# Reordering the loads, casts and weight parts of an attention and max-out kernel's first 60 microseconds

## Chip, cores and metric

The kernel runs on one core of one Trainium2 chip. The metric is the device time of one execution in microseconds (us).

## What is computed

The reference is a softcap attention followed by a feed-forward layer with a maximum of two products. Cut to what matters:

```python
batch, n_heads, seq, head_dim = (8, 12, 448, 64)          # q, k, v: float32, cap = 30
scores = (1 / sqrt(head_dim)) * q @ k.T                   # per batch and head, 448 x 448
scores = cap * tanh(scores / cap)
attn = softmax(scores)
x = (attn @ v).transpose(0, 2, 1, 3).reshape(3584, 768)   # heads side by side
out = maximum(x @ w1, x @ w2) @ w_out                     # w1, w2: 768 x 1024, w_out: 1024 x 768
```

## The kernel before

**Units and groups.** Two heads of one batch element make a unit ("pair"); there are 48 of them. Three units make a **group**, the portion in which q, k and v are loaded: groups 0 to 15, called the first, second, third and so on. The attention loop takes two units per step `t`, so a step may need two groups: step 3 is the first that reads group 2 (units 6 and 7), and step 4 the first that reads group 3 (unit 9).

**Road of q and k.** `load(g, what)` (L113) issues the DMAs from SP's queue into a float32 staging tile, `kr`, `qr` or `vr` in the profile. `raw_of` (L105) takes that tile from a pool: two buffers each for k and q, used in turn, and a single one for v. For groups 0 and 1 a load is one DMA, from group 2 on it is two (q) or three (k, v): the first 384 rows of each head, then the other 64. `cast` (L140) converts the tile to bf16, most often on GpSimd; k and q go into `kqf`, one of two tiles by the group's parity, v into `vp` and `vl`, also two of each. Then k and q have to be transposed to have the head dimension on the partitions. For groups 0 and 1 TensorE does it (`transposes`, L255, L267 and L268), from group 2 on a DMA does, `cross(g)` (L271), issued from SP, from `kqf` into `qkT`.

**Road through attention.** `scores(t, p)` (L282, matmuls of L295 and L300) computes a quarter of a step's scores in PSUM and lets ScalarE take the tanh (L301, L303). `ex` (L305, L308) takes the exponential. `add` (L316) forms partial sums of exponentials on VectorE, `total` (L337) sums over the keys on TensorE and inverts on VectorE, `values` (L358) multiplies with v, and `normalize` (L386) writes x, transposed, as `xT`.

**Road of the weights.** The maximum is computed as `x @ w2 + relu(x @ (w1 - w2))`, so `wd = w1 - w2` and `wm = w2 @ w_out` are needed. w1 and w2 come in six parts each. `load_w2(c)` (L209) and `load_wo(f)` (L200) are issued from GpSimd's queue and convert to bf16 on the way; w2's parts land in a tile that the profile calls `gT`. `load_w1(c)` (L214) is issued from SP's queue in float32, into tiles called `osb` and `xT`. `subtract(c)` (L218, L219) forms one part of wd on GpSimd. `turn_w2(c)` (L223) transposes w2 on TensorE, and `premultiply` (L231, L237) and `premultiply_first` (L518, L524) multiply it with w_out.

**The feed-forward part.** `moe(b)` (L392, matmuls of L400, L412 and L415) works on one batch element after the other.

**What sets the order.** Each engine executes its instructions in the order in which the program issues them, and this order is written out by hand: first a prologue for steps 0 to 2 (L474 to L592), then the loop over `t`. Matmuls of the weights and of the feed-forward part are kept as generators in a list and drawn into the attention's gaps by `F(n)` (L444), n at a time, counted and not timed. Three queues matter around the change: SP's instructions (loads of q, k, v, w1, the transposes, later the stores), GpSimd's instructions (issues of w2 and w_out, casts, subtractions), and the DMA engines, which serve both. An instruction that waits, for a buffer or for data, holds everything behind it on its engine.

**Order on the two engines in question.** On SP: k and q of groups 0 and 1, v of group 0, v of group 1 (its one buffer is free when group 0's v is cast, by GpSimd and VectorE), k and q of group 2, w1 parts 0 and 1, `cross(2)`, w1 parts 2 to 5, k, q of group 3, v of group 2, and in step 2 `cross(3)`. On GpSimd, after the first w2 parts and w_out: cast of group 1's k and q, w2 parts 2 to 5, half of group 0's v, group 1's v, group 2's k and q, subtractions 0 and 1, subtractions 2 and 3, group 3's k and q, subtractions 4 and 5, group 2's v.

Of the kernel before, what the change touches and what calls it, by code (L numbers as in the profile page):

```python
# [10 lines left out]
def kernel(  # L11
# [11 lines left out]
    nc = tc.nc  # L23
    f32 = mybir.dt.float32
# [4 lines left out]
    B, H, S, D = q.shape  # L29
# [3 lines left out]
    P = 128  # L33
    KC, FC = DM // P, DF // P
    NP = H // 2
    N = B * NP
    L = 3
    NQ = N // 2
    Q0 = 4 * P
    NJ = 3  # L40
# [55 lines left out]
    raw = {}  # L96
# [4 lines left out]
    def rows(t, b, h0, h1):  # L101

        return t[b, h0:h1, :, :].rearrange("h (r j) d -> (h r) (j d)", j=R7)

    def raw_of(g, what):  # L105
        if (g, what) not in raw:
            raw[g, what] = stage.tile([P, 2 * L * NJ * D + (2 * L if what == "q" else L) * D], f32, name=what + "r", bufs=1 if what == "v" else 2)
        t = raw[g, what]
        m = t[:, : 2 * L * NJ * D].rearrange("p (h c) -> p h c", c=NJ * D)
        l = t[:, 2 * L * NJ * D :].rearrange("p (h d) -> p h d", d=D)  # L110
        return t, m, l

    def load(g, what, n0=0, n1=L):  # L113
        b, p = divmod(g * L, NP)
        h0, h1 = 2 * (p + n0), 2 * (p + n1)
        src = {"k": k, "q": q, "v": v}[what]
        t, m, l = raw_of(g, what)
        if g < NT:
            nc.sync.dma_start(
                out=t[:, n0 * S : n1 * S].rearrange("p (n c) -> p n c", c=S),  # L120
                in_=rows(src, b, h0, h1).rearrange("(n p) c -> p n c", p=P),
            )
            return
        nc.sync.dma_start(
            out=m[:, 2 * n0 : 2 * n1, :],
            in_=src[b, h0:h1, 0 : NJ * P, :].rearrange("h (p j) d -> p h (j d)", j=NJ),
        )
        if what == "q":
            nc.sync.dma_start(
                out=l[half(b), 2 * n0 : 2 * n1, :],  # L130
                in_=src[b, h0:h1, NJ * P : S, :].rearrange("h p d -> p h d"),
            )
        else:
            for par in range(2):
                nc.sync.dma_start(
                    out=l[64 * par : 64 * par + 64, n0:n1, :],
                    in_=src[b, h0 + par : h1 : 2, NJ * P : S, :].rearrange("h p d -> p h d"),
                )

    def cast(eng, g, what, n0=0, n1=L, halves=(0, 1)):  # L140

        b = g * L // NP
        x, m, l = raw_of(g, what)
        if what == "v" and g < NT:

            x = x[:, : L * S].rearrange("p (n c) -> p n c", c=S)
            for h in halves:
                r = slice(64 * h, 64 * h + 64)
                for a in range(2):
                    eng.tensor_copy(  # L150
                        vp[g % 2][64 * a : 64 * a + 64, h::2, :, :].rearrange("p n j d -> p n (j d)"),
                        x[r, :, NJ * D * a : NJ * D * (a + 1)],
                    )
                eng.tensor_copy(vl[g % 2][r, :, r], x[r, :, 2 * NJ * D :])
            return
        if what == "v":
            eng.tensor_copy(  # L157
                vp[g % 2][:, 2 * n0 : 2 * n1, :, :].rearrange("p h j d -> p h (j d)"), m[:, 2 * n0 : 2 * n1, :]
            )
            for par in range(2):  # L160
                r = slice(64 * par, 64 * par + 64)
                eng.tensor_copy(vl[g % 2][r, n0:n1, r], l[r, n0:n1, :])
            return
        if g < NT:

            x = x[:, n0 * S : n1 * S].rearrange("p (n c) -> p n c", c=S)
            if what == "q":
                eng.tensor_copy(flat(g)[:, n0:n1, Q0 : Q0 + S], x)
                return
            eng.tensor_copy(flat(g)[:, n0:n1, : NJ * P], x[:, :, : NJ * P])  # L170
            for par in range(2):
                r = slice(64 * par, 64 * par + 64)
                eng.tensor_copy(kf[g % 2][r, n0:n1, 3, r], x[r, :, NJ * P :])
            return
        o = b % 2 if what == "q" else 0
        t = (kf if what == "k" else qf)[g % 2]
        eng.tensor_copy(  # L177
            t[:, n0:n1, o : o + NJ, :].rearrange("p n j (h d) -> p n h j d", h=2),
            m[:, 2 * n0 : 2 * n1, :].rearrange("p (n h) (j d) -> p n h j d", h=2, d=D),
        )  # L180
        if what == "q":
            eng.tensor_copy(
                t[half(b), n0:n1, 3 * (1 - o), :],
                l[half(b), 2 * n0 : 2 * n1, :].rearrange("p (n h) d -> p n (h d)", h=2),
            )
        else:
            for par in range(2):
                r = slice(64 * par, 64 * par + 64)
                eng.tensor_copy(t[r, n0:n1, 3, r], l[r, n0:n1, :])
# [19 lines left out]
    def load_w2(c):  # L209
        nc.gpsimd.dma_start(out=w2b[:, c, :], in_=x_rows(moe_w2, c))  # L210
# [7 lines left out]
    def subtract(c, eng=nc.vector):  # L218
        eng.tensor_sub(wd_sb[:, c, :], w1_in[c], w2b[:, c, :])  # L219
# [51 lines left out]
    def cross(g):  # L271

        nc.sync.dma_start_transpose(
            out=qkT_of(g).rearrange("p n j c -> p (n j) c"), in_=kqf[g % 2].rearrange("p n j c -> p (n j c)")
        )
# [228 lines left out]
    ex(0, 3)  # L504
    cast(nc.gpsimd, 1, "k")
    cast(nc.gpsimd, 1, "q")
    for c in range(2, KC):
        load_w2(c)
    cast(nc.gpsimd, 0, "v", halves=(1,))
    load(1, "v")  # L510
    load(2, "k")
    load(2, "q")
    load_w1(0)
    load_w1(1)

# [2 lines left out]
    def premultiply_first(f0, f1):  # L518
        if f0 == 0:
            first[0] = pv_psum.tile([P, 512], f32, name="pv")  # L520
            first[1] = pv_psum.tile([P, 512], f32, name="ss")
        for f in range(f0, f1):
            for half in range(2):
                nc.tensor.matmul(  # L524
                    first[half][:, : DM // 2],
                    w2T[0][:, f * P : (f + 1) * P],
                    wo_sb[:, f, half * (DM // 2) : (half + 1) * (DM // 2)],
                    start=(f == 0), stop=(f == FC - 1),
                )
        if f1 == FC:  # L530
            for half in range(2):
                nc.vector.tensor_copy(
                    wm_sb[:, 0, half * (DM // 2) : (half + 1) * (DM // 2)], first[half][:, : DM // 2]
                )
# [7 lines left out]
    scores(1, 0)  # L542
    transposes(3)
    cast(nc.vector, 0, "v", halves=(0,))
    cast(nc.gpsimd, 1, "v")
    cast(nc.gpsimd, 2, "k")
    cast(nc.gpsimd, 2, "q")
    premultiply_first(0, 2)
    scores(1, 1)
    ex(1, 0)  # L550
# [6 lines left out]
    scores(1, 3)  # L557
    ex(1, 2)
    cross(2)
    for c in range(2, KC):  # L560
        load_w1(c)
    load(3, "k")
    load(3, "q")
    load(2, "v")
    premultiply_first(6, 8)
    for c in range(1, KC):
        if c + 1 < KC:
# [9 lines left out]
    for t in range(1, NQ):  # L577
        i = 2 * t
        more = t + 1 < NQ
        if t > 1 and more:  # L580
            scores(t + 1, 0)
        if t > 1:
            ex(t, 3)
            F(6)
        if t in crosses:
            cross(crosses[t])
        if t == 2:
            subtract(2, nc.gpsimd)
            subtract(3, nc.gpsimd)
            cast(nc.gpsimd, 3, "k")  # L590
            cast(nc.gpsimd, 3, "q")
            cross(3)  # L592
            subtract(4, nc.gpsimd)
            subtract(5, nc.gpsimd)
        if t == 3:
            cast(nc.gpsimd, 3, "v")
        if t > 2:
            extra(i)
        F(8 if t > 1 else 0)
        add(t, 1, 0)  # L600
        F(2 if t > 1 else 0)
        if more:
            scores(t + 1, 1)
            ex(t + 1, 0)
        F(4)
        add(t, 1, 1)
        F(4)
        if t == 2:
            cast(nc.gpsimd, 2, "v")
            load(3, "v")  # L610
        add(t, 0, 2)
        F(4)
        add(t, 1, 2)
        F(4)
        if more:
            scores(t + 1, 2)
            ex(t + 1, 1)
            F(5)
            add(t + 1, 0, 0)
        if t == 1:  # L620
            subtract(0, nc.gpsimd)
            subtract(1, nc.gpsimd)
        if t == 2:
            extra(4)
            extra(5)
        if t > 2:
            extra(i + 1)
        F(5)
        total(t)
        if more:  # L630
            scores(t + 1, 3)
            ex(t + 1, 2)
            add(t + 1, 0, 1)
        else:
            F(12)
        normalize(t, values(t))
        if t % 3 == 2:
            fill_q.append(moe(t // 3))
        F(3)
# [34 lines left out]
```

## Time and profile before

| What | Value |
|---|---|
| Time, median of 13 runs (range) | 364.16 us (362.19 to 366.56) |
| Profiled execution, its time | 366.56 us |
| Its span, first to last instruction | 364.8 us |
| Mean granted TensorE clock | 0.991 |
| Busy: TensorE, ScalarE, VectorE, GpSimd | 336.2, 281.7, 239.2, 112.5 us |
| DMA bytes moved, mean rate | 61.79 MB, 169 GB/s |
| Last exponential of ScalarE ends | 307.7 us |

A profile row names the engine (PE is TensorE, ACT ScalarE, DVE VectorE, POOL GpSimd, SP the engine that issues most DMAs, with a q for its issues), the line of the kernel, the operation, and the tiles as out<-in with their shapes. In a timeline the row starts with its start and duration in us, and its bracket holds the idle time of the engine before it and what ended that. The granted clock is a share of TensorE's full clock. The DMA share is the busy share of the 16 DMA engines, which can come out somewhat above 1.

### The profile page before, as it was taken

The page shows a single profiled execution, that of the slowest core. Times are in us where ns is not written, and L with a number is a line of the kernel's source. Part 1 is how long each engine was busy: PE and PEld are TensorE (multiplying, and loading weights), DVE is VectorE, ACT ScalarE, POOL GpSimd, SP SyncE. Part 2 cuts the span into 40 slices and gives each one's busy share as a digit, 9 for nine tenths or more (in the row PEclk, how much of TensorE's full clock was granted, in tenths as well). Part 3 has the DMA queues.
Part 4 walks back from the last instruction along what each step waited for, and adds up shares of the span by engine and source line. Part 5 has one row for each costly group of instructions (what it writes and reads, how often), then busy time and mean ns, then how long its engine had stood idle before and what let it go on. Part 6 is the DMA issues. An engine that isn't in the chain of part 4 may idle for free.

```text
span 364.8 us, 6775 instructions
## 1 busy us (share of the span) xinstructions
PE 336.2 (92%) x2710; PEld 163.6 (45%) x2710; DVE 239.2 (66%) x410; ACT 281.7 (77%) x265; POOL 112.5 (31%) x154
## 2 busy tenths in 40 slices
PE   4889695989979999999999999999999999899996
PEld 2434252434534444344534454445444545455563
DVE  4254465886778686788678767886787667833421
ACT  4998696779989999899998999999999999000000
POOL 6624759471181109110911091109210100000000
PEclk9998999899999999999999999999999999999999
DMA  7999696896778486949593963995392111012022
GB/s 259 247 214 340 128 359 154 237 287 159 215 209 192 100 257 207 231 94 265 163 244 78 260 183 96 260 275 160 92 245 78 43 45 75 13 45 87 0 88 86
DMA packets 103200, 61.79 MB, mean 169 GB/s; under 512 B 62336, under 2 KB 98176, under 8 KB 103168
## 3 DMA queue, kind: packets, MB, share of 16 engines
q1 hardware_dynamic: 101216, 58.21, 57.3%
q0 software_dynamic: 1952, 3.15, 4.7%
q8 instruction: 21, 0.34, 0.4%
q14 instruction: 11, 0.09, 0.1%
HBM read 42.47 MB, written 11.01 MB: 147 GB/s over the span
## 4 chain that ended last, share of the span: by engine, by line
PE 42%; ACT 33%; DVE 12%; DMA 3%; SPq 3%; issue 2%; POOL 2%; ACTq 0%; POOLq 0%; DVEq 0%
PE mm L400 16%; ACT expo L308 15%; ACT tanh L301 15%; PE mm L415 8%; PE mm L412 6%; PE s L300 4%; ACT tanh L303 3%; DVE esum L327 3%; DVE esum L329 3%; PE ss L366 2%; DVE esum L331 2%; DVE gT L404 2%; PE pv L366 2%; DMA qkT<-kqf 1%; DVE osb L419 1%
## 5 line engine op out<-in xcount | busy, mean ns | idle before, releaser
L308 ACT ACTIVATE expo<-tanh 128x1792 bf16<-128x1792 bf16 (+1 forms) x96 | 144.8, 1509 | 0.1
L301 ACT ACTIVATE tanh<-s 128x896 bf16<-128x896 f32 x144 | 124.3, 914 | 20.4 <-PE s L300 18.5
L415 PE MATMUL mm<-wo_sb,gT 128*128 128x384 bf16 x448 | 86.3, 327 | 0.0
L400 PE MATMUL mm<-xT,wd_sb 128*128 128x448 bf16 x384 | 79.9, 353 | 4.6 <-DVE gT L404 2.3
L412 PE MATMUL mm<-wm_sb,xT 128*128 128x384 bf16 x336 | 66.8, 326 | 0.7 <-DVE osb L419 0.7
L157 POOL CAST vp<-vr 128x1152 bf16<-128x1152 f32 x14 | 16.6, 1184 | 142.3 <-PE ss L366 115.7
L415 PEld LDWEIGHTS <-gT 128*128 128x128 bf16 x448 | 42.1, 98 | 35.1 <-issue 8.8
L419 DVE COPY osb<-mm 128x384 f32<-128x384 f32 x56 | 31.0, 554 | 38.2 <-PE mm L415 38.0
L400 PEld LDWEIGHTS <-wd_sb 128*128 128x128 bf16 x384 | 35.9, 98 | 44.0 <-issue 13.4
L300 PE MATMUL s<-qkT 64*128 64x448 bf16 x288 | 43.1, 369 | 12.8 <-DMA qkT<-kqf 7.6
L329 DVE TENSOR_TENSOR esum<-expo 128x896 bf16<-128x896 bf16 x42 | 32.7, 779 | 29.9 <-ACT expo L308 29.2
L404 DVE TENSOR_SCALAR gT<-mm 128x448 bf16<-128x448 f32 x64 | 39.5, 620 | 13.5 <-PE mm L400 13.1
L412 PEld LDWEIGHTS <-xT 128*128 128x128 bf16 x336 | 31.5, 98 | 26.0 <-issue 5.8
L327 DVE TENSOR_TENSOR esum<-esum,expo 64x896 bf16<-64x896 bf16 x42 | 31.1, 740 | 1.1
L331 DVE TENSOR_TENSOR esum<-esum,expo 128x896 bf16<-128x896 bf16 x42 | 29.6, 704 | 0.2
L303 ACT ACTIVATE tanh<-s 128x896 bf16<-128x896 f32 x24 | 22.0, 916 | 6.4 <-PE s L295 5.9
L300 PEld LDWEIGHTS <-qkT 64*128 64x128 bf16 x288 | 9.7, 95 | 36.1 <-issue 25.4
L366 PEld LDWEIGHTS <-vp 128*32 128x32 bf16 x576 | 13.5, 97 | 19.9 <-issue 12.5
L352 DVE STREAM_TRANSPOSE st<-ss 128x448 f32<-128x448 f32 x24 | 15.5, 646 | 9.4 <-PE ss L350 5.4
L366 PE MATMUL ss<-expo,vp 128*32 128x448 bf16 x288 | 18.0, 355 | 2.2 <-DVE st L352 2.1
L366 PE MATMUL pv<-expo,vp 128*32 128x448 bf16 x288 | 18.6, 365 | 0.0
L177 POOL CAST kqf<-qr 128x1152 bf16<-128x1152 f32 x14 | 17.4, 1240 | 1.7 <-DMA qr<-in_q_dram 0.9
(69 smaller groups left out, 263.7 us busy)
## 6 DMA issues: line engine op xcount, KB each, us to landing
kr<-in_k_dram SPq DMA_DIRECT2D x14, 576.0 KB, 4.8
qr<-in_q_dram SPq DMA_DIRECT2D x14, 576.0 KB, 5.9
vr<-in_v_dram SPq DMA_DIRECT2D x14, 576.0 KB, 5.2
out_dram<-osb SPq DMA_DIRECT2D x20, 384.0 KB, 2.7
out_dram<-osb SPq DMA_DIRECT2D x16, 192.0 KB, 2.8
osb<-in_moe_w_dram SPq DMA_DIRECT2D x4, 512.0 KB, 5.5
gT<-in_moe_w_dram POOLq DMA_DIRECT2D x6, 256.0 KB, 9.9
wo_sb<-in_moe_w_out_dram POOLq DMA_DIRECT2D x4, 384.0 KB, 15.2
```

What stands on the lines that cost most here:

```text
L300: nc.tensor.matmul(s[:, h, :S], k0[r, j * P : (j + 1) * P], qTn[r, :])
L301: nc.scalar.activation(tanh[t, p][:, 2 * m : 2 * m + 2, :], s[:, :, :S], AF.Tanh, scale=scale / cap)
L308: nc.scalar.activation(expo[t, p], tanh[t, p][:, 0:n, :], AF.Exp, scale=float(cap))
L327: nc.vector.tensor_add(d, d, expo[t, 2][r, :, :])
L329: nc.vector.tensor_add(d, e_of(t, ab, 1 if ab else 0), e_of(t, ab, 2 if ab else 1))
L331: nc.vector.tensor_add(d, d, e_of(t, ab, 0 if ab else 2))
L366: nc.tensor.matmul(ps[r, :S], vp[g % 2][:, 2 * n + h, j, u::2], e_of(t, ab, j)[:, h, :], start=(j == 0), stop=False,)
L400: nc.tensor.matmul(ps[:, :S], wd_sb[:, c, f * P : (f + 1) * P], x[:, c, cs], start=(c == 0), stop=(c == KC - 1))
L404: nc.vector.tensor_relu(g[:, f, cs], ps[:, :S])
L412: nc.tensor.matmul(ps[:, : DM // 2], x[:, c, ts], wm_sb[:, c, hs], start=(c == 0), stop=False)
L415: nc.tensor.matmul(ps[:, : DM // 2], g[:, f, ts], wo_sb[:, f, hs], start=False, stop=(f == FC - 1))
L419: nc.vector.tensor_copy(osb[:, hs], ps[:, : DM // 2])
```

## The change

The third group's k and q get the second buffer of their pool instead of the first: an additional tile is taken from the pool and left unused, so that group 2 shares buffers with group 1, and group 3 with group 0. Group 2's q and k are loaded ahead of group 1's v and cast ahead of it. w2's parts 4 and 5 are issued behind these casts. Group 3's k and q are loaded ahead of w1's parts 2 to 5, and cast behind subtractions 0 and 1, which move from step 1 into the prologue; the other four subtractions come behind those casts, in step 2. No instruction is added or removed.

```diff
+    def raw_tile(what):
+        return stage.tile(
+            [P, 2 * L * NJ * D + (2 * L if what == "q" else L) * D], f32, name=what + "r", bufs=1 if what == "v" else 2
+        )
...
-            raw[g, what] = stage.tile([P, 2 * L * NJ * D + (2 * L if what == "q" else L) * D], f32, name=what + "r", bufs=1 if what == "v" else 2)
+            raw[g, what] = raw_tile(what)
...
     def load(g, what, n0=0, n1=L):
         b, p = divmod(g * L, NP)
+        if g == 2 and what != "v":
+            raw.setdefault((2, what, "skipped"), raw_tile(what))
...
     cast(nc.gpsimd, 1, "k")
     cast(nc.gpsimd, 1, "q")
-    for c in range(2, KC):
-        load_w2(c)
+    load_w2(2)
+    load_w2(3)
     cast(nc.gpsimd, 0, "v", halves=(1,))
+    load(2, "q")
+    load(2, "k")
     load(1, "v")
-    load(2, "k")
-    load(2, "q")
     load_w1(0)
     load_w1(1)
...
     cast(nc.vector, 0, "v", halves=(0,))
+    cast(nc.gpsimd, 2, "q")
+    cast(nc.gpsimd, 2, "k")
+    load_w2(4)
+    load_w2(5)
     cast(nc.gpsimd, 1, "v")
-    cast(nc.gpsimd, 2, "k")
-    cast(nc.gpsimd, 2, "q")
...
     cross(2)
+    load(3, "k")
+    load(3, "q")
     for c in range(2, KC):
         load_w1(c)
-    load(3, "k")
-    load(3, "q")
     load(2, "v")
+    subtract(0, nc.gpsimd)
+    subtract(1, nc.gpsimd)
+    cast(nc.gpsimd, 3, "k")
+    cast(nc.gpsimd, 3, "q")
...
         if t == 2:
-            subtract(2, nc.gpsimd)
-            subtract(3, nc.gpsimd)
-            cast(nc.gpsimd, 3, "k")
-            cast(nc.gpsimd, 3, "q")
             cross(3)
-            subtract(4, nc.gpsimd)
-            subtract(5, nc.gpsimd)
+            for c in range(2, KC):
+                subtract(c, nc.gpsimd)
...
-        if t == 1:
-            subtract(0, nc.gpsimd)
-            subtract(1, nc.gpsimd)
```

## The prediction

> **What bounds the kernel now.** I read the page's busy shares first. TensorE is busy for nine tenths of the span, and its instruction order is fixed in the program, so the question is where its few idle microseconds lie.
>
> ```profile
> PE 336.2 (92%) x2710; PEld 163.6 (45%) x2710; DVE 239.2 (66%) x410; ACT 281.7 (77%) x265; POOL 112.5 (31%) x154
> ```
>
> The TensorE timeline (start, duration, instructions, idle time before them and what ended it) shows two long holes, both in the first 70 us and both ended by a transpose that the DMA engines make, qkT<-kqf: 3.48 us before 44.06 (the third group's scores) and 4.08 us before 62.86 (the fourth group's).
>
> ```profile
> 40.09 0.49 PE L237 MATMUL mm<-wo_sb,w2T 128*128 128x384 bf16 x2
> 44.06 0.55 PE L300 MATMUL s<-qkT 64*128 64x448 bf16 x4 [3.48 <-DMA qkT<-kqf]
> ...
> 62.86 0.55 PE L300 MATMUL s<-qkT 64*128 64x448 bf16 x2 [4.08 <-DMA qkT<-kqf]
> 63.34 4.11 PE L237 MATMUL mm<-wo_sb,w2T 128*128 128x384 bf16 x16
> ```
>
> The ScalarE timeline has the same holes (2.70 and 2.87) and a third, 1.97, behind those 16 slow matmuls.
>
> ```profile
> 44.52 1.73 ACT L301 ACTIVATE tanh<-s 128x896 bf16<-128x896 f32 x2 [2.70 <-PE s L300]
> ...
> 63.46 0.92 ACT L301 ACTIVATE tanh<-s 128x896 bf16<-128x896 f32 x1 [2.87 <-PE s L300]
> ...
> 67.93 0.92 ACT L303 ACTIVATE tanh<-s 128x896 bf16<-128x896 f32 x1 [1.97 <-PE s L295]
> ```
>
> Why are the transposes late? The GpSimd and SP timelines answer (an SP row is an issue).
>
> ```profile
> 31.99 1.37 POOL L150 CAST vp<-vr 64x576 bf16<-64x576 f32 x2 [8.84 <-DMA vr<-in_v_dram]
> ...
> 35.53 1.14 POOL L177 CAST kqf<-kr 128x1152 bf16<-128x1152 f32 x1
> ...
> 39.24 4.21 POOL L219 TENSOR_TENSOR wd_sb<-osb,gT 128x1024 bf16<-128x1024 f32 x2
> ```
>
> ```profile
> 3.69 19.86 SPq L119 DMA_DIRECT2D vr<-in_v_dram  x2
> 23.65 0.43 SPq L124 DMA_DIRECT2D kr<-in_k_dram  x1
> ...
> 39.18 3.07 SPq L273 DMA_TRANSPOSE qkT<-kqf  x1
> ...
> 57.54 3.12 SPq L273 DMA_TRANSPOSE qkT<-kqf  x1
> ```
>
> SP sits until 23 us on the second v load, waiting for its only buffer; k and q of group 2 are issued behind it. GpSimd waits 8.84 us for that v, casts it, and only then casts k and q: they end at 39.16, and the transpose leaves at 39.18. The table of windows shows the DMA engines nearly idle meanwhile (last two columns: DMA share, GB/s), after being full from 2 to 36 us:
>
> ```profile
> 36.00:38.00 2.00, 2.00 (x30) 1.09 (x29) 0.56 (x1) 1.97 (x3) 1.88 (x4) 1.00 0.14 55
> 38.00:40.00 2.00, 2.00 (x36) 0.79 (x36) 1.79 (x4) 1.97 (x2) 1.85 (x3) 1.00 0.03 8
> ```
>
> **What the Trainium skill says.** "DMA: Bandwidth & Descriptors", section "Queues, rings and completion order": each DMA engine takes turns between queues, packet by packet, and works one queue in order. The trace agrees: group 0's v, alone on SP's queue but beside the weights on GpSimd's, took 17.5 us to land, group 1's q 12.1, and group 2's last q, alone, 2.0 after k. "TensorE: Matmul & The Clock Gate", section on the HAM clock gate: an idle window of some 3.4 us halves the clock. The trace agrees: granted clock 0.50 at 64 to 66 us, and 16 matmuls of L237 take 4.04 us there against 2.60 for 15 at 55.88. "SBUF — State Buffer", section "Who interferes with whom": VectorE and GpSimd share a port that one holds for a whole instruction. At 59.67 a sum of L329 took 2.60 us beside the subtractions; elsewhere 0.62.
>
> **The change, part by part.**
>
> *Group 2 ahead of v.* The load of q is now issued when GpSimd's casts of group 1 end, 16.65 us, not 23.65: staging in group 1's buffers adds that wait on SP. Behind it stand only k and group 1's v, and v waits until 23 anyway, so the wait costs nothing if it ends by then. From the trace's issue-to-landing times, the landings before are: w2 parts 26.1, 27.5, 29.4, 31.5; v 32.0; k 33.9; q 35.9; w1 parts 36.9, 38.1. Two loads leave the front: w2's last two parts (their predecessors took 2.6, they took 4.0 beside v; I take 3) and v (same bytes as q: 2). So k lands at 35.9 - 3 - 2 = 31, estimate; bounds 29.5, and 34 because it landed by then with v ahead. q's cast (1.15 + 0.51) fits under k's transfer; k's takes 1.14 + 0.75 = 1.9. The transpose can leave at 33, not 39.18.
>
> It will not land 6 us earlier, though: v and two w1 parts are ahead of it in SP's queue, and w2's last parts now compete. The DMA work is the same; only the idle 3.7 us of the two windows can go. 44.0 - 3.7 = 40.3; I take 41, bounds 39.5 and 43.
>
> *Cost at the start.* q's packets now alternate with w_out's from about 18 us (data flows some 1 us after an issue: the transpose of 39.18 fills the engines from 40). Its last two parts landed at 23.0 and 24.9, TensorE used them at 23.10 and 25.02: no slack. If they slow by a quarter of 18 to 24.9, that is 1.7 us; TensorE has 1.40 idle before 27.24, so 0.5 remains (bounds 0; 2.2 if the gap at 21 us also keeps the clock at half, doubling the some 4.8 us of matmuls up to 28.4, less what the idle time covers). TensorE asks for the scores at 40.58 + 0.5 = 41.1 and resumes at 41.3 instead of 44.06: **2.7 gained**, 2.5 on ScalarE.
>
> *w2's last parts and v behind.* GpSimd: 33 + issue of two parts 1.1 + v casts 3.45 = 37.6; before, 35.5. values(1) reads v at 38.4 + 0.5, so this is covered by 1.3 us; beyond that TensorE waits. The w2 parts land near 38; their transposes are wanted at 44.
>
> *Group 3 ahead of w1.* Its four k and q issues pass w1's four on SP. k and q land 4.2 after the first transpose, 45.2; GpSimd has by then done subtractions 0 and 1 (41.8) and ends the casts at 47, ten earlier than 57.5. But the second transpose still stands behind w1's four parts and v on SP, so the DMA work sets it: 62.8 less 3.7 and less the 1.7 idle between 56 and 60 us (shares 0.39 and 0.75) gives 57.4; I take 57.2, bounds 55.5 and 59. TensorE now asks at 58.77 - 2.7 = 56.1: 1.1 us of waiting for 4.1, **3.0 gained**. A wait of 1 us no longer empties a clock window: **1.4 gained**. ScalarE: 2.5 + 2.87 + some 1.9.
>
> *Subtractions and helpers.* The unused tiles of group 2 and the new helper issue no instruction, and the swap of k and q moves none to another queue: nothing. All six subtractions stay on GpSimd; four follow group 3's casts, 47 + 8.4 = 55.4 (before 61.8). L400 needs them at 67.83 - 7: covered. group 2's v cast ends near 57.7 for a use at 63.4: covered.
>
> *Given back.* VectorE has about 16 us of work from 59.67 to 77 (some 3 of it blocked by GpSimd), much of it done in the holes; squeezed into 12 to 13 us it must cost something. I take 1 us (0 to 2).
>
> Sum: 2.7 + 3.0 + 1.4 - 1 = 6.1, say **6.2** with the slightly larger ScalarE figure. The rest, to 307.7 where ScalarE ends, keeps its order and shifts. The profiled execution had a span of 364.8 and took 366.56, 2.40 above the median: 360.4 there, **358.0** against the median.
>
> **Rivals.**
>
> *Half of it* (0.20): transposes at the late bounds, 43 and 59; 1.0 and about 2 gained, no more: 361.2. For it: loads ahead in SP's queue are unchanged in bytes. Against: the idle DMA windows.
>
> *Nothing* (0.07): the DMA engines, full to 36 us, fill the hole with w2's parts and the start-up loss takes the rest: 364. This includes the case that group 2's load does not really move ahead.
>
> *Slower* (0.11): q and k starve beside the weights on GpSimd's queue, since by their access patterns they move in pieces of 64 and 192 floats, 256 and 768 B, against 2 KB of a w2 row, and turns are counted in packets. GpSimd then stands at q's cast with w2's parts and v's cast behind it. With k at 38 the v casts end near 44.5, values(1) waits 6 us and the scores start near 46.7, 2.6 late, which the second hole repays; so 38 is the point from which it decides, and at 40 the kernel takes about 366.5. Against: the weights had nearly landed by 31.5 even when four w2 parts stood ahead.
>
> **How the numbers follow.** The main case has 0.62, its own range 355.8 to 360. Range 355.8 (nearly all waits gone, nothing given back) to 361.9 (half of it). A measurement can tell 0.3%, 1.1 us, from no change: faster 0.80, same 0.08, slower 0.12.
>
> **What would show it.** Right: the first transpose issued near 33 and the second near 51; TensorE waits for qkT<-kqf of about 1.5 us in sum for 7.6; no half clock after 60 us; DMA share near 1 at 36 to 40. Wrong: k of group 2 landing after 34, a wait of values(1) for GpSimd's vl, TensorE at half clock past 25 us, or ScalarE gaps after 65 us as long as the ones removed.

## The result: 1.1% slower

The changed kernel took 367.61 us in the median of 11 runs (365.59 to 370.8), the kernel before 364.01 of 48 (361.25 to 366.85): ratio 1.0112, 95% interval 1.0086 to 1.0138. The prediction was 358.0, range 355.8 to 361.9. Ratios and intervals, here and below, leave out the few executions that lay more than 1.5% above the fastest of the same kernel; medians do not. The profiled execution took 368.63 us (before 366.56), with a span of 366.8 (before 364.8) and a mean TensorE clock of 0.980 (before 0.991).

The lines below answer to those of the prediction. The change adds 7 to the line numbers: L280 is the transpose, L307 the scores, L308 the tanh, L184 and L196 the casts of k, L226 the subtraction, L244 the product of w2 and w_out. First the busy times, nearly those of before:

```profile
PE 335.0 (91%) x2710; PEld 163.1 (44%) x2710; DVE 236.8 (65%) x410; ACT 281.6 (77%) x265; POOL 113.0 (31%) x154
```

The TensorE timeline (start, duration, instructions, idle time before them and what ended it):

```profile
39.59 0.49 PE L244 MATMUL mm<-wo_sb,w2T 128*128 128x384 bf16 x2
49.39 0.93 PE L307 MATMUL s<-qkT 64*128 64x448 bf16 x4 [9.31 <-DMA qkT<-kqf]
50.25 4.66 PE L244 MATMUL mm<-wo_sb,w2T 128*128 128x384 bf16 x14
```

The hole before the third group's scores has grown from 3.48 to 9.31 us; the clock is halved behind it, so that 14 matmuls of L244 take 4.66 us; at full clock 15 took 2.60. The fourth group's hole (4.08) is gone. ScalarE shows the same: one gap of 8.92 and one of 2.17, for 2.70, 2.87 and 1.97.

```profile
50.05 1.73 ACT L308 ACTIVATE tanh<-s 128x896 bf16<-128x896 f32 x2 [8.92 <-PE s L307]
55.52 1.73 ACT L308 ACTIVATE tanh<-s 128x896 bf16<-128x896 f32 x2 [2.17 <-PE s L307]
```

The GpSimd timeline shows k of the third group cast early, at 31.77 for 35.53, and w2's last two parts issued at 33.56:

```profile
31.77 1.15 POOL L184 CAST kqf<-kr 128x1152 bf16<-128x1152 f32 x1 [0.97 <-DMA kr<-in_k_dram]
32.87 0.75 POOL L196 CAST kqf<-kr 64x192 bf16<-64x192 f32 x2
33.56 1.07 POOL L217 DMA_DIRECT2D gT<-in_moe_w_dram  x2
...
50.91 1.14 POOL L184 CAST kqf<-kr 128x1152 bf16<-128x1152 f32 x1 [8.47 <-DMA kr<-in_k_dram]
```

The SP timeline has the transpose at 33.64, 5.5 us earlier than before. Its issue takes 7.77 us for 3.07.

```profile
9.18 0.37 SPq L131 DMA_DIRECT2D qr<-in_q_dram  x1
9.59 0.74 SPq L136 DMA_DIRECT2D qr<-in_q_dram  x1
10.37 8.68 SPq L131 DMA_DIRECT2D kr<-in_k_dram  x1
...
33.64 7.77 SPq L280 DMA_TRANSPOSE qkT<-kqf  x1
...
55.05 6.96 SPq L280 DMA_TRANSPOSE qkT<-kqf  x1
```

The chain that ended last, asked for the stretch 14 to 70 us (start, duration, what), names what became of the 5.5 us: the transpose takes 15.70 us, before 4.8.

```profile
33.61 0.03 POOL gT L217
33.64 15.70 DMA qkT<-kqf
```

And the table by stretches (busy time of the five engines, clock, DMA share, GB/s) shows that the DMA engines were not idle in that time. They were busy throughout and moved little:

```profile
36.00:38.00 2.00, 1.77 (x28) 0.68 (x31) 1.21 (x4) 1.97 (x2) 1.85 (x5) 1.00 0.97 95
38.00:40.00 2.00, 2.00 (x32) 0.82 (x29) 1.54 (x3) 1.97 (x3) 1.91 (x2) 1.00 1.37 183
40.00:42.00 2.00, 0.08 (x1) 0.00 (x0) 0.85 (x2) 1.13 (x2) 2.00 (x2) 1.00 1.34 75
42.00:44.00 2.00, 0.00 (x0) 0.00 (x0) 0.00 (x0) 0.00 (x0) 0.44 (x1) 1.00 1.19 102
44.00:46.00 2.00, 0.00 (x0) 0.00 (x0) 0.00 (x0) 0.00 (x0) 0.00 (x0) 0.69 1.28 85
```

Before, the transpose had the stretch from 40 to 44 nearly to itself (w1's parts were issued behind it from 42.30), and moved more:

```profile
40.00:42.00 2.00, 0.58 (x7) 0.17 (x3) 1.50 (x3) 1.82 (x3) 2.00 (x2) 1.00 0.93 178
42.00:44.00 2.00, 0.00 (x0) 0.00 (x0) 0.00 (x0) 0.00 (x0) 1.45 (x1) 1.00 1.16 231
```

**Where the 2.0 us of span come from.** The start lost 0.48 us (the scores of L300 at 28.05 are now at 28.53), but this is made up: TensorE reaches the third group's scores at 40.08, before at 40.58. Up to there the clock was halved once in both, before at 28.5 to 32.0 and now at 17.5 to 20.9. The first hole then costs 5.83 more and the absence of the second saves 4.08. Behind its hole TensorE works 5.6 us at half clock (49.39 to 55.0), before 3.2 (62.86 to 66.1), which makes some 1.2 us more, an estimate. Together that is -0.5 + 5.8 - 4.1 + 1.2 = 2.4. Measured: the first feed-forward matmul starts at 70.15 for 67.83, the last exponential at 308.85 for 306.78, +2.3 and +2.1. So the loss is complete by 70 us. This is the account of the two profiled executions, 2.1 us apart; the medians lie 3.6 us apart, and the rest has no profile.

**One part of the change does not happen.** The load of the third group's q is issued at 9.18, when the first group's q has been cast, not behind the second group's casts (which ended at 16.65 before, and now end at 17.66). So the third group still stages in the first group's buffers: the tile that was taken from the pool and never written or read did not shift them. The run "staged" below does what was described.

### The profile page after: what moved, and what is told of

It reads as the page before. It is cut to its first block, busy times and chain, and to the rows that moved or that the text cites. A ratio compares the mean times of both kernels' runs of the same rounds, so it can differ in the third digit from the quotient of the medians.

```text
span 366.8 us, 6778 instructions
## 1 busy us (share of the span) xinstructions
PE 335.0 (91%) x2710; PEld 163.1 (44%) x2710; DVE 236.8 (65%) x410; ACT 281.6 (77%) x265; POOL 113.0 (31%) x154
## 4 chain that ended last, share of the span: by engine, by line
PE 45%; ACT 27%; DVE 12%; DMA 7%; SPq 5%; issue 2%; ACTq 0%; POOL 0%; DVEq 0%; POOLq 0%
PE mm L407 16%; ACT expo L315 13%; ACT tanh L308 12%; PE mm L422 10%; PE mm L419 7%; DMA qkT<-kqf 4%; PE s L307 4%; DMA kr<-in_k_dram 3%; DVE esum L336 3%; ACT tanh L310 3%; SPq L131 2%; DVE esum L334 2%; PE ss L373 2%; SPq L142 2%; DVE gT L411 2%
## 5 line engine op out<-in xcount | busy, mean ns | idle before, releaser
L308 ACT ACTIVATE tanh<-s 128x896 bf16<-128x896 f32 x144 | 124.2, 914 | 24.3 <-PE s L307 22.2
L307 PE MATMUL s<-qkT 64*128 64x448 bf16 x288 | 42.5, 366 | 14.3 <-DMA qkT<-kqf 9.3
L336 DVE TENSOR_TENSOR esum<-expo 128x896 bf16<-128x896 bf16 x42 | 30.4, 725 | 29.7 <-ACT expo L315 29.0
L307 PEld LDWEIGHTS <-qkT 64*128 64x128 bf16 x288 | 9.5, 95 | 37.0 <-issue 24.7
L184 POOL CAST kqf<-kr 128x1152 bf16<-128x1152 f32 x14 | 17.0, 1215 | 11.2 <-DMA kr<-in_k_dram 10.7
L184 POOL CAST kqf<-qr 128x1152 bf16<-128x1152 f32 x14 | 17.5, 1251 | 7.9 <-DMA qr<-in_q_dram 7.1
```

Of the source, the lines that this page charges most:

```text
L184: eng.tensor_copy(t[:, n0:n1, o : o + NJ, :].rearrange("p n j (h d) -> p n h j d", h=2), m[:, 2 * n0 : 2 * n1, :].rearrange("p (n h) (j d) ...
L307: nc.tensor.matmul(s[:, h, :S], k0[r, j * P : (j + 1) * P], qTn[r, :])
L308: nc.scalar.activation(tanh[t, p][:, 2 * m : 2 * m + 2, :], s[:, :, :S], AF.Tanh, scale=scale / cap)
L336: nc.vector.tensor_add(d, e_of(t, ab, 1 if ab else 0), e_of(t, ab, 2 if ab else 1))
```

## The experiments

**Theory (collision):** w2's parts 4 and 5, now issued at the same moment as the transpose, hold it up. **Rivals:** the early loads, the staging, or the fourth group's loads ahead of w1 do it.

**1. w2_back: the changed kernel with w2's parts 4 and 5 in their old place.**

```diff
-    load_w2(2)
-    load_w2(3)
+    for c in range(2, KC):
+        load_w2(c)
...
-    load_w2(4)
-    load_w2(5)
```

> The changed kernel, but with w2's parts 4 and 5 issued where they were, right behind parts 2 and 3. Collision theory (the third group's DMA transpose runs at the same time as w2's last two parts, which convert on the way from GpSimd's queue, and both crawl): the transpose lands 5 to 6 us after its issue instead of 15.7, TensorE's hole before the third group's scores falls from 9.3 us to under 2, and the time to 358 to 361 us. Early-load theory (k and q of the third group, issued at 9 us, hold back the weights and SP, and all that follows is late): the hole stays above 7 us, the time at 366 to 368.

Measured: 362.45 us, ratio 0.9954 (0.9928 to 0.9979). The transpose leaves at 36.04 and lands 5.5 us later; TensorE has no wait for it, only 1.45 us for v ahead of it. The early loads and those of the fourth group ahead of w1 are still in this kernel, so moving the two parts alone makes the difference between a gain and a loss. But the time is above what was expected, for the *fourth* group's transpose, issued at 48.83 behind loads on its own queue, lands 12.7 us later (SP timeline, then TensorE timeline):

```profile
36.04 3.37 SPq L280 DMA_TRANSPOSE qkT<-kqf  x1
...
48.83 9.35 SPq L280 DMA_TRANSPOSE qkT<-kqf  x1
```

```profile
61.62 0.55 PE L307 MATMUL s<-qkT 64*128 64x448 bf16 x2 [5.22 <-DMA qkT<-kqf]
```

**2. w2_only: the kernel before, with only w2's parts 4 and 5 moved** behind the third group's casts.

> The kernel before, with w2's parts 4 and 5 alone moved behind the casts of the third group's k and q, so that they are issued together with its transpose; nothing else is changed. Collision theory: the transpose takes 12 to 16 us from issue to landing instead of 4.8, TensorE's hole of 3.5 us grows to 7 to 10, the time is 367 to 371 us. Early-load theory: moving the two parts away only frees the front, the casts end some 3 us sooner, and the time is 361 to 363.

Measured: 368.39 us, ratio 1.0116 (1.0066 to 1.0166), the loss of the whole change. TensorE timeline:

```profile
51.34 0.93 PE L300 MATMUL s<-qkT 64*128 64x448 bf16 x4 [10.28 <-DMA qkT<-kqf]
```

The transpose is issued at 35.98 and lands 15.3 us later. The first of the two w2 parts lands 5.3 us after its issue, the second 14.0: the delay is on both queues. With experiment 1 this is the cause from both sides: taken out, the loss goes; put in alone, it comes.

**3. g3_only: the kernel before, with the fourth group's part alone** (its loads ahead of w1, its casts behind subtractions 0 and 1).

```diff
-    for c in range(2, KC):
-        load_w1(c)
     load(3, "k")
     load(3, "q")
+    for c in range(2, KC):
+        load_w1(c)
...
```

> The kernel before with the fourth group's part of the change alone: its k and q loaded ahead of w1's parts 2 to 5, cast behind subtractions 0 and 1, the other four subtractions behind those casts. Collision theory: this part is innocent; the first hole stays at 3.5 us, the second (4.1 us) shrinks to 0 to 2 and the half clock behind it goes, the time is 359 to 362. The rival that the fourth group's transpose is set by the order of the DMA queue alone and gains nothing: the second hole stays at 3 us or more, 363 to 365.

Measured: 363.35 us, ratio 0.9979 (0.9953 to 1.0005), no difference that can be told. The first transpose is as before (issued 38.53, lands 4.7 later). The second leaves at 51.25, 6 us earlier, with w1 and v still under way on its own queue, and lands 10.0 us later for 5.3; its hole is 1.54 for 4.08. The last load ahead of it lands at 57.15 and the transpose 4.1 us after that; before, these were 58.55 and 4.3. So it mainly waits its turn.

**4. staged: the changed kernel, with the third group really in the second group's buffers** (two fixed tiles each for k and q).

> The changed kernel with the third group's k and q really placed in the second group's buffers (four fixed staging tiles), so that their load waits for the casts of the second group at some 17.6 us; in the changed kernel the load left at 9.2 us behind casts of the first group. Collision theory: no cure, since w2's parts 4 and 5 still meet the transpose: a hole of 7 us or more, 365 to 369. Early-load theory: the weights are no longer held back, the hole falls below 4 us, 358 to 363.

Measured: 367.58 us, ratio 1.0097 (1.0067 to 1.0127). The load of q is issued at 18.59, k is cast at 31.59 (31.77 without), the transpose leaves at 33.46 and takes 17.8 us, the hole is 10.05. The time is that of the changed kernel: where the third group is staged makes no difference that can be told.

**5. plain_pool: the kernel before, with two plain loads of 256 KB added** (the left half of w2's parts 4 and 5, read in float32 without conversion into a tile that nobody reads), on GpSimd's queue behind the third group's casts.

```diff
...
+    for c in range(4, 6):
+        nc.gpsimd.dma_start(out=extra_in[:, c - 4, :], in_=x_rows(moe_w2, c)[:, : DF // 2])
```

> The kernel before, with two additional loads on GpSimd's queue behind the casts of the third group's k and q: the left half of w2's parts 4 and 5, in float32 without conversion, into a tile that nothing reads (256 KB each, rows of 2 KB, as many pieces and written bytes as the two parts that the change moved). If the conversion on the way is what does not mix with a transpose, the transpose lands 5 to 8 us after its issue and the time is 364 to 367 us. If any traffic of a second queue beside a transpose is, it lands after 12 to 16 us, the hole of 3.5 us grows past 8, and the time is 368 us or more.

Measured: 365.22 us, ratio 1.0036 (1.0013 to 1.006). The transpose lands 8.2 us after its issue, the hole is 6.46. That looked like "conversion is the culprit", but these loads read half the bytes of the two parts. Runs 12 to 14 take up this question.

**6 and 7. g2_only and g2_again: the kernel before, with the third group's part alone**: q and k loaded and cast ahead of v, w2 unmoved. The same program twice, on two chips.

```diff
-    load(1, "v")
-    load(2, "k")
     load(2, "q")
+    load(2, "k")
+    load(1, "v")
...
-    cast(nc.gpsimd, 1, "v")
-    cast(nc.gpsimd, 2, "k")
     cast(nc.gpsimd, 2, "q")
+    cast(nc.gpsimd, 2, "k")
+    cast(nc.gpsimd, 1, "v")
```

> The kernel before with the third group's part of the change alone: its q and k loaded and cast ahead of the second group's v; w2's parts and the fourth group stay as they were. If the step that failed in the prediction was only the traffic beside the transpose, the first hole shrinks to 1.5 us or less, the second stays near 4 us since its transpose still leaves on quiet DMA engines, and the time is 360.5 to 362.5. If loading early costs as much as it gains, 363.5 to 365.

> The same program as the kernel before with the third group's part alone, beside the two splits on one chip: 360 to 361.8 us by its first runs. If its gain was chance, 363 to 364.

Measured: 360.83 us, ratio 0.9911 (0.988 to 0.9942), and 361.63 us, ratio 0.9915 (0.9882 to 0.9948). This is the time that was expected, and the program is **faster than both kernels**. SP timeline of g2_again, the transpose with w1's parts 2 to 5 behind it:

```profile
35.41 3.60 SPq L273 DMA_TRANSPOSE qkT<-kqf  x1
39.06 1.04 SPq L216 DMA_DIRECT2D osb<-in_moe_w_dram  x2
...
54.53 3.08 SPq L273 DMA_TRANSPOSE qkT<-kqf  x1
```

The first leaves at 35.41 and lands 5.7 us later, at 41.1, before TensorE asks, although w1's parts 0 and 1, ahead of it on its own queue, land only at 36.65 and 38.25; the second lands 4.8 later. The DMA engines are again full for most of this stretch, but at 1.5 and 2.7 times the rate of the changed kernel:

```profile
38.00:40.00 2.00, 2.00 (x33) 0.93 (x34) 0.94 (x2) 1.97 (x3) 1.91 (x3) 1.00 1.25 277
40.00:42.00 2.00, 2.00 (x37) 0.91 (x35) 1.83 (x5) 1.97 (x3) 2.00 (x2) 1.00 0.88 200
```

In TensorE's timeline the first hole has gone and the second is 1.65. The last exponential starts at 301.06, 5.7 us earlier than before; the two holes give 3.48 + 2.43 = 5.9. That compares two profiled executions, of 360.84 and 366.56 us; the medians on this chip lie only 2.8 us apart. In the profile of g2_only, an execution of 366.11 us, the transposes take 7.1 and 5.3 us and the holes are 1.66 and 2.98, so one program varies by more than 1 us in a hole.

```profile
59.33 0.36 PE L300 MATMUL s<-qkT 64*128 64x448 bf16 x2 [1.65 <-DMA qkT<-kqf]
```

**8. g3_cross_first: as 3, with the second transpose issued ahead of w1's parts 2 to 5 and v**, so that no load is under way on its queue.

> The kernel before with the fourth group's part alone, and its transpose issued on SP ahead of w1's parts 2 to 5 and of the third group's v, which then leave behind it in step 2. No load is then in flight beside the transpose. If loads ahead of a transpose in its own queue slow it too, it now lands 4.7 to 5.5 us after its issue instead of 10.0 without this step, the second hole is under 0.5 us and its half clock gone, and the time is 359 to 361.5. If they only delay it by their own bytes, moving them behind gives the same hole and pushes the subtractions late, 363 to 365.

Measured: 370.45 us, ratio 1.0176 (1.0141 to 1.021): both sides missed. The transpose lands 7.1 us after its issue, and its hole is 0.63, near the 0.5 hoped for. But the subtractions wait for w1 (GpSimd timeline), end at 71.5 instead of 61.8, and the feed-forward part waits 1.27, 0.79, 2.10 and 1.90 us in four pieces, the last three of them for the subtractions (TensorE timeline):

```profile
61.59 4.98 POOL L219 TENSOR_TENSOR wd_sb<-osb,gT 128x1024 bf16<-128x1024 f32 x2 [8.56 <-DMA osb<-in_moe_w_dram]
```

```profile
69.10 0.56 PE L400 MATMUL mm<-xT,wd_sb 128*128 128x448 bf16 x1 [2.10 <-POOL wd_sb L219]
71.56 1.68 PE L400 MATMUL mm<-xT,wd_sb 128*128 128x448 bf16 x4 [1.90 <-POOL wd_sb L219]
```

**9. both_cross_first: the same order together with the third group's part**, staged as described, w2 unmoved.

> Both parts of the change with transposes alone on the DMA engines: w2's parts 4 and 5 issued with parts 2 and 3, the third group really staged in the second group's buffers, and the fourth group's transpose ahead of w1's parts 2 to 5 and of the third group's v. Theory that traffic beside a transpose was all that undid the change: both holes nearly vanish, 6 to 8 us, 356.5 to 359. Rival, that w1 and v now come too late for the subtractions and for values(3): a new wait of 2 us or more on L407's weights or on vp near 60 to 66 us, 360 to 363.

Measured: 366.67 us, ratio 1.0076 (1.0048 to 1.0105). The second transpose lands 4.7 us after its issue without a hole (the first 7.3, hole 1.88), and again the subtractions come late: GpSimd waits 8.10 for w1, the feed-forward part 3.09 + 0.41 + 0.51. Only the 0.41 is put down to a subtraction; the other two end with VectorE's casts to wm_sb, which stand behind sums that take 2.42 and 1.97 us beside the subtractions (0.62 before, when the subtractions were done). Right in kind for the rival, worse in size than its 360 to 363.

**10 and 11. split_a and split_b: in between.** Both start from w2_back. Split_a puts w1's parts 2 and 3 ahead of the second transpose and 4 and 5 behind it; split_b puts parts 2 and 3 ahead of the fourth group's loads as well, and subtraction 2 ahead of its casts.

> The changed kernel with w2's parts 4 and 5 issued with parts 2 and 3, and on SP, behind the third group's transpose: k and q of the fourth group, w1's parts 2 and 3, the fourth group's transpose, w1's parts 4 and 5, v of the third group. Theory that the second hole is cured when the transpose leaves on quiet engines, and that the failure of the kernel with the transpose ahead of all w1 parts was GpSimd's late subtractions: transpose lands within 6 us, the second hole under 1 us, subtractions end by 61 us, L407's wait for wd_sb under 1 us, 357.5 to 360. Rival, that parts 2 and 3 are still in flight and slow the transpose: second hole 2 us or more, 361 to 363.

> As the kernel with the fourth group's transpose between w1's parts 3 and 4, but with w1's parts 2 and 3 ahead of the fourth group's k and q too, and subtraction 2 ahead of their casts: the casts are then the last to wait, and the transpose leaves when nothing is in flight. Quiet-engine theory: it is issued near 49.5 us, lands within 5.5 us, second hole under 1 us, 357.5 to 360. Rival, that GpSimd's chain (subtraction 2, casts, three subtractions) becomes the bound: the transpose is issued after 51 us, second hole 1 to 3 us, or L407 waits 2 us or more for wd_sb, 361 to 364.

Measured: split_a 361.56 us, ratio 0.9937 (0.9909 to 0.9965). Its transposes land 7.4 us (hole 2.00) and 4.6 us (no hole) after their issue, and GpSimd waits 2.72 for w1. Its second transpose is as the theory had it, the time as the rival had it. Split_b 363.62 us, ratio 0.9985 (0.9961 to 1.0008); 7.2 and 7.3 us, holes 1.77 and 1.34, and GpSimd waits 6.48 for w1's last parts: the rival's case. Split_a cures w2_back's second transpose, and it cannot be told from the third group's part alone (medians 361.56 and 361.63 on the same chip).

**12. w2_one: as 2, with part 5 alone moved.**

> The kernel before with only w2's part 5 moved behind the casts of the third group's k and q: half of the converting traffic beside the transpose. If the slow-down follows the amount of that traffic, the transpose lands 9 to 11 us after its issue (4.8 without any, 15.3 with two parts), the hole is 6 to 7.5 us, and the time 365 to 367. If any converting part stalls it for as long as both, 14 us or more and 367.5 to 369.

Measured: 365.22 us, ratio 1.0017 (0.9995 to 1.0039); the transpose lands 7.9 us after its issue, hole 5.52. Less than was expected, and less than half of the effect of two: it lands 3.1 us later than before's 4.8 for one part, 10.5 later for two.

**13 and 14. plain_full and cast_full: conversion or amount?** As 5, with the whole of parts 4 and 5 (512 KB each as read), in one kernel into a float32 tile and in the other into a bf16 tile.

> The kernel before with two loads of 512 KB each added on GpSimd's queue behind the casts of the third group's k and q: the whole of w2's parts 4 and 5, read without conversion into a tile that nobody reads (w2's own parts stay where they were, so the output is unaffected). It reads as many bytes as the two moved parts did. If conversion on the way is what holds the transpose up, it lands within 10 us of its issue, TensorE waits 5 to 8 us for it, and the time is 365 to 367. If the amount read on a second queue decides, it lands 12 us or more after its issue, as the moved parts made it, and the time is 368 to 371.

> The same two added loads of 512 KB, at the same place, but into a bf16 tile that nobody reads, so that they convert on the way. If conversion is what holds the transpose up, it lands 14 us or more after its issue, the wait of TensorE is 9 to 11 us and the time 368 to 371, while the loads without conversion stay below 10 us. If the amount read decides, both kernels are alike.

Measured: plain_full 373.58 us, ratio 1.0249 (1.0186 to 1.0312), transpose landing 14.9 us after its issue; cast_full 370.58 us, ratio 1.0145 (1.0081 to 1.0208), 13.6 us. TensorE timelines of the two, in this order:

```profile
53.27 0.93 PE L301 MATMUL s<-qkT 64*128 64x448 bf16 x4 [12.61 <-DMA qkT<-kqf]
```

```profile
52.30 0.93 PE L301 MATMUL s<-qkT 64*128 64x448 bf16 x4 [11.20 <-DMA qkT<-kqf]
```

Conversion is not the cause: without it the wait is no shorter. The delay goes with the amount on the other queue. The first transpose of every run, sorted by what was read beside it:

| Read on GpSimd's queue beside it | Transpose, issue to landing |
|---|---|
| nothing, and no load ahead under way on SP's queue (before, g3_only, g3_cross_first) | 4.7 to 4.8 us |
| nothing, but w1's parts 0 and 1 ahead on SP's queue, landing up to 2.9 us after its issue (w2_back, g2_again, g2_only, split_b, both_cross_first, split_a) | 5.5, 5.7, 7.1, 7.2, 7.3, 7.4 us |
| 512 KB (w2_one: 128 rows of 4 KB; plain_pool: 256 of 2 KB) | 7.9, 8.2 us |
| 1 MB (w2_only, cast_full, plain_full; with w1's parts ahead as well: the changed kernel, staged) | 15.3, 13.6, 14.9; 15.7, 17.8 us |

The traces also hold every single packet that the DMA engines moved, and these show where the second 512 KB costs more than the first. The transpose is 3072 packets of 256 B. With nothing beside it, the first of them starts 1.3 us after the issue and the last 2.9 to 3.0 us later (before, g3_only, g3_cross_first). With one w2 part beside it (w2_one) the first packet starts only after 3.5 us, when 103 of that part's 128 packets have started, and the transpose then runs for 3.8 us, nearly undisturbed. With two loads of 512 KB (w2_only, cast_full, plain_full) it starts after 3.6 to 3.7 us as well, but now the second load runs beside it, and it takes 9.5 to 11.2 us. Its packets then add up to 136 to 159 us of time, summed over the 16 engines, against 55 to 60 when it is alone.

## Why the prediction was wrong, point by point

- **Start of the kernel**, 0.5 us lost: right at 28 us, 0.48, with w_out's last two parts landing 1.1 and 1.8 us later (I took 1.7). It did not last: TensorE asks for the third group's scores at 40.08, not at 41.1. The 17.5 us of group 0's v, which I read as the price of sharing with GpSimd's queue, contain loads on SP's own queue as well: the last k or q ahead of it lands at 15.23, v at 21.22.
- **k of the third group lands at 31, transpose leaves at 33**: right, cast at 31.77 and issue at 33.64; not for the whole reason given, since the load did not wait for the second group's casts (16.65) but went out at 9.18. Staged shows that this is immaterial. That the two w2 parts hold the front up was right too: with them back in place the transpose leaves at 36.04, 2.4 us later, near the 3 us that I took for them.
- **The transpose lands at 41, bounds 39.5 and 43: this step failed.** "The DMA work is the same; only the idle 3.7 us of the two windows can go" took the DMA engines for a resource whose times add up, whatever runs together. It landed at 49.3. An estimate: 1 MB at the 379 GB/s that the engines moved at 34 to 36 us of before takes 2.8 us, so that adding up gives 4.8 + 2.8 = 7.6; measured are 13.6 to 17.8. What the Trainium skill says of turns between queues, packet by packet ("DMA: Bandwidth & Descriptors", section "Queues, rings and completion order"), fits a transpose that is slowed, but neither it nor my bounds held a factor of three. I had written that w2's parts "now compete", and added 0.7 us for it (41 for 40.3).
- **2.7 us gained at the first hole**: 5.8 lost. Without w2's move the hole is gone (w2_back, g2_again), a gain of up to the full 3.48.
- **v behind**, casts done at 37.6, covered by 1.3: nearly, they end at 38.14 and TensorE waits 0.23 for v. In w2_back, split_a and both_cross_first, where the casts of k come later, it waits 1.45.
- **Fourth group: casts end at 47, transpose issued at 51, landing 57.2**: 55.0, 55.05 and 65.7, all held back by the first transpose. Where that is not so (w2_back), the issue is at 48.83, and it lands at 61.6, outside the bounds of 55.5 and 59. This is the second term that was mis-sized. That the loads ahead of it on SP's queue come first was right: in g3_only, the changed kernel, staged and w2_back it lands 4.0 to 4.2 us after the last of them, before 4.3. What failed is that these loads would be done so much sooner: in w2_back the last lands at 57.57, 1.0 us earlier than before, though the first transpose landed 2.5 us earlier. The 1.7 us of idle time that I took out of 56 to 60 us came back as slow stretches (101 GB/s at 54 to 56, at a DMA share of 1.78). Why is open. With the transpose ahead of most of these loads it takes 4.6 to 7.3 us (runs 8 to 11), but then w1 is late.
- **3.0 gained at the second hole and 1.4 of half clock**: TensorE no longer waits there, only because everything comes later; the half clock went from 63 to 45 us on and costs some 1.2 us more instead. The idle window of 3.4 us that I counted with also does not explain all of before: the clock is halved at 28.5 to 32.0 behind waits of only 1.40 and 0.44 us, and stays full behind the hole of 3.48.
- **Subtractions end at 55.4**: 64.3, still covered. That this cover is thin, runs 8 and 9 showed.
- **1 us given back on VectorE**: not separated. In g2_again TensorE waits 1.40 and 0.60 us for gT at 76 to 79 us, against 0.21 and 0.92 at 74 to 81 before; the difference is of this size, but w2_back has only 0.16 there.
- **The slower rival** (q and k starve, deciding point k at 38) named the wrong victim: k came at 31.8. It had the right place, GpSimd's queue beside SP's, but I let the weights delay the loads and not the transpose.

Not settled is what happens in the DMA engines when a transpose and plain loads of another queue run side by side, so that the packets of both take longer. The table of amounts speaks against the conversion, and rows of 2 and 4 KB give nearly the same delay for 512 KB, so that bytes seem to decide there rather than rows. One or two profiles stand behind each of these numbers, and the same program gave 5.7 and 7.1 us in two of them.

## What to carry to other kernels

Price a DMA transpose by what else will be in flight when it leaves, not by its duration in a trace where it ran alone. Here, loads ahead of it on its own queue cost about the time until they had landed, but 1 MB beside it on another queue made it about three times as long, far more than the two transfers add up to. When something critical moves forward, ask what the same edit moves into its place: here no version was clearly faster than the third group's part alone, without the transfers that were moved out of the way. Test a bundle by its parts; one part held a gain of 0.9%, one the whole loss.

## What had not been expected of the hardware

- A high DMA share can mean little work: 1.19 to 1.37 at 75 to 183 GB/s from 38 to 46 us, against 1.25 at 277 GB/s in g2_again at 38 to 40, with the transpose and loads of its own queue.
- It matters on which queue the other loads stand. Behind loads on its own queue the transpose landed 2.8 to 4.8 us after the last of them (first transposes of the six runs in the table's second row; second ones of g3_only, w2_back, staged and the changed kernel), no more than it takes from its issue when it is alone. Beside 1 MB on GpSimd's queue it took 13.6 to 17.8.
- The issue of a transpose lengthens with its trouble: 3.1 us when it is alone, 4.3 to 10.8 beside loads on GpSimd's queue, 6.4 to 9.4 behind w1's parts and v on its own. Behind it stand all later loads of SP, so that the fourth group's k was cast at 50.91 although it stood ahead of w1.
